# Fewer VectorE instructions ahead of the three accumulations in step 23 of each expert, and the two parts of k and v added before the fold's transposes

## The chip, the core and the metric

One core of a Trainium2 chip runs the whole program. Its engines are TensorE (PE, with its weight loads PEld), VectorE (DVE), ScalarE (ACT), GpSimd (POOL) and SyncE (SP, which issues the DMAs). The metric is the device time of one execution in microseconds (us); of several runs the median is given.

## The reference, cut to what matters

Attention over 32 memory slots per head, and then a mixture of four dense experts on its output:

```python
a = softmax(phi)                                  # over the sequence, 8 batches x 8 heads
k_m = einsum('bhsm,bhsd->bhmd', a, k)             # 32 x 64 per head
v_m = einsum('bhsm,bhsd->bhmd', a, v)
attn = softmax(scale * q @ k_m^T)                 # over the 32 slots
x = (attn @ v_m), heads side by side              # 4608 x 512
p = domain_probs / domain_probs.sum(-1)
out = sum over e of p[:, e] * (relu(x @ w1[e]) @ w2[e])   # 4 experts, 512 -> 1024 -> 512
```

## The kernel before

Every large product is made from two parts of each operand, a rounded "hi" and the rest "lo" (hi*hi + hi*lo + lo*hi). ACT writes a hi with a copy that rounds; DVE then writes the lo as the difference.

**The main loop.** The batches are taken in four pairs (k). For each pair and each of four experts (e) there are 32 steps: 16 for the even batch, 16 for the odd one, each in two halves of the sequence with eight steps (j = 0 to 7, one for each 128 of the expert's 1024 hidden columns). That makes 512 steps; "step 23" below is the eighth and last step of the odd batch's first half, in each of the 16 blocks of 32. In a step PE runs `first_mm(s + 2)`, the six products of the first layer of two steps ahead (lines 416 to 418, tile `p1`, shown as `p`), then the side work that was planned for the step, then `second(s)`, three products for each output tile of 128 tokens (lines 457 to 459, tile `p2`, also shown as `p`). ACT (L432) and DVE (L438) turn `p1` into `h`, or into `hm` for the 64 tokens that the two batches share.

**The output tiles.** A half has two output tiles, the odd batch's first half three (t0 = 5, 6 and 4). A tile collects its products over eight steps in one of four PSUM buffers (tag `p2`), and at j = 7 DVE adds it, times the token's probability, to `acc` or `accm` (L474; L472 for the first expert). The buffers are taken in turn: tile 8, which begins in step 24 as the second tile there, takes the buffer of tile 5, which ends in step 23. DVE runs its instructions in the order written, so tile 5's accumulation comes after all side work that was planned for DVE in step 23.

**Side work.** Meanwhile the next expert's weights are split (`w`, L597/601 and L625/629), the products of v and w1 are made and split (`pv` at L360 to 362, `vw` at L372 by ACT and L378 by DVE), and the attention of later batches runs. A planner writes this order: every operation has an engine, a cost and the operations that it depends on; `place` puts it into the first step in which `room(eng, s)` holds what is already there and its cost (in PE columns), one step later than anything it needs from another engine. `BUSY` names steps of a block (22 to 31) in which attention work is not put. Within a step, up to a cost of 2300, DVE's side work stands ahead of the step's `h` (only what needs nothing of another engine in that step), and the rest behind it; the accumulations are last.

**The fold.** For batches 2 to 7, `kv_ops` leaves for each pair of heads (hp) a PSUM tile `x` of 128 rows by 256 columns: two parts (hi and lo of the softmax weights), each for two heads, as rows; k and v as columns. `kv_out` scales and copies it to SBUF (`xs`, ACT, L234). `kv_fold` turns it with PE transposes (L244, tile `kvp`), four for two head pairs (one group, g). `kv_pick_ops` takes the blocks that are wanted: two copies of the first part into `kvT` (L920, one on ACT, one on DVE), and two additions of the second part (L925, DVE). There are two groups in each of six batches, twelve in all. Batches 0 and 1 use `kv_out`, `kv_fold` and `kv_pick`, and are scheduled by hand.

Of the kernel before, what the change touches and what calls it, by code (L numbers as in the profile page):

```python
# [9 lines left out]
F32 = mybir.dt.float32  # L10
F32R = mybir.dt.float32r
AF = mybir.ActivationFunctionType
ALU = mybir.AluOpType
# [3 lines left out]
B, H, S, D, M = 8, 8, 576, 64, 32  # L17
N, DM, E, F = 4608, 512, 4, 1024
P = 128
# [4 lines left out]
NJ = F // P  # L24
# [5 lines left out]
STAGE = 5  # L30
TH = S // 2
KVS = 2
AHEAD = 2


# [12 lines left out]
def body(ctx: ExitStack, tc: tile.TileContext, qm, qt, qh, kv, kvt, phi, phn, prob, w1, w2, out):  # L48
    nc = tc.nc
    pool = lambda name, **k: ctx.enter_context(tc.tile_pool(name=name, bufs=1, **k))  # L50
    const, wp, work, att = pool("const"), pool("wp"), pool("work"), pool("att")
    psum = pool("psum", space=PSUM)

    ident = const.tile([P, P], F32, name="ident")
    make_identity(nc, ident)
    kvT = [const.tile([P, 2, NP, 2 * M], F32, name=f"kvT{i}") for i in range(2)]
# [74 lines left out]
    st = {}  # L131
# [71 lines left out]
    def kv_split(b, hp, raw, c2, eng):  # L203
        tag = {"tag": "kvs", "bufs": KVS} if b else {"tag": "vw1", "bufs": 5}
        t = att.tile([P, 4 * TH] if b else [P, 1024], F32R, name="kvs", **tag)
        t = t[:, :1024].rearrange("p (s f) -> p s f", s=2)
        t = t.rearrange("p s (i d) -> p s i d", i=2)
        src = raw[:, 2 * c2:2 * c2 + 2].rearrange("p c w d -> p c (w d)")
        nc.scalar.copy(t[:, 0], src)
        eng.tensor_sub(t[:, 1], src, t[:, 0].bitcast(F32))  # L210
        st["kvs", b, hp, c2] = t
# [16 lines left out]
        )  # L228

    def kv_out(b, hp):  # L230
        xs = att.tile([P, 2 * P], F32, name="xs", tag="xs", bufs=2)
        x = st["x", b, hp // 2][:, hp % 2, :]
        if b > 1:
            nc.scalar.activation(xs, x, AF.Copy, scale=st["rz", b][:, hp:hp + 1])  # L234
        else:
            nc.scalar.copy(xs, x)
        st["xs", b, hp] = xs

    def kv_fold(b, hp):
        g = hp // 2  # L240
        if hp % 2 == 0:
            st["kvp", b, g] = psum.tile([P, 2, 2, P], F32, name="kvp", tag="pm", bufs=4)
        for w in range(2):
            nc.tensor.transpose(  # L244
                st["kvp", b, g][:, hp % 2, w, :], st["xs", b, hp][:, w * P:(w + 1) * P], ident
            )
# [154 lines left out]
    def where(s):  # L401
        k, s = divmod(s, PAIR)
        e, s = divmod(s, STEPS)
        odd, s = divmod(s, 2 * NJ)
        half, j = divmod(s, NJ)
        return k, e, odd, half, j
# [14 lines left out]
    def first_hi(s, ps):  # L421
        _, _, odd, _, j = where(s)
        h = work.tile([P, 2, 2 * P], F32R, name="h", tag="h", bufs=AHEAD + 2)
        parts = [(h, slice(0, 2 * P), slice(0, 2 * P))]
# [91 lines left out]
    OA = lambda n, fn, *deps, **k: Op("ACT", 350 + 1.9 * n, fn, deps, **k)  # L516
    OD = lambda n, fn, *deps, **k: Op("DVE", 290 + 2.42 * n, fn, deps, **k)
    OG = lambda n, fn, *deps, **k: Op("POOL", 300 + 2 * n, fn, deps, **k)
    OT = lambda n, fn, *deps, **k: Op("PE", n, fn, deps, **k)
# [5 lines left out]
    def room(eng, s):  # L525
        odd, half, j = where(s)[2:]
        n = HALF[odd][half]
        wide, tiles_ = n == WIDE, 2 + (odd == 1 and half == 0)
        length = 6 * n + 3 * DM * tiles_ + used["PE", s]
        if eng == "PE":  # L530
            return 2400
        if eng == "POOL":
            return 3000
        if eng == "SP":
            return 4
        if eng == "ACT":
            return 0.95 * length - 840 - 470 * wide
        done = (3 if odd == 1 and half == 1 else 2) if j == 0 else 0
        return 0.95 * length - 910 - 445 * wide - 1640 * done

    busy = [True]

# [13 lines left out]
    def place(ops, lo=MANUAL, bank=None):  # L556
        while True:
            done, after = [], defaultdict(int)
            for op in ops:
                s = max([op.lo, lo, MANUAL, after[op.eng]] + [d.step + lag for d, lag in op.deps])  # L560
                while not fits(op, s):
                    s += 1
                op.step = after[op.eng] = s
                charge(op, s)
                done.append(op)
            span = range(ops[bank[0]].step, ops[bank[1]].step + 1) if bank else ()
            if all(banks[s] < 2 and not (busy[0] and s % STEPS in BUSY) for s in span):
                break
            for op in done:
                charge(op, op.step, -1)  # L570
            lo = max(lo, ops[0].step) + 1
        for s in span:
            banks[s] += 1
        for op in ops:
            todo[op.step][op.eng].append(op)
            assert op.late is None or op.step <= op.late
        return ops
# [9 lines left out]
        def give(self, op):  # L587
            self.last.append(op)

    w1_ring, kvs_ring = Ring(4), Ring(KVS)  # L590

    def plan_w1(e, fh, g, lo):
        key = ("w1", e, fh, g)
# [47 lines left out]
    last, VTS = {}, {}  # L641
# [15 lines left out]
    def prev(name, lag=1):  # L657
        d = last.get(name)
        return d and (d, lag)

    def plan_att(b, lo):
# [99 lines left out]
        def kv_ops(hp):  # L761
            key = ("kv", b, hp)

            def k_hi(c2):
                t = att.tile([P, 4 * TH], F32R, name="kvs", tag="kvs", bufs=KVS)
                t = t[:, :1024].rearrange("p (s i d) -> p s i d", s=2, i=2)
# [22 lines left out]
        at_kv = max(lo, lw[0].step - 2)  # L789
        for g in range(2):  # L790
            u = kv_ops(2 * g)
            u += kv_ops(2 * g + 1)
            us = u if g == 0 else us + u
            xa = [OA(256, lambda i=i, g=g: kv_out(b, 2 * g + i), u[-1], prev("fold")) for i in range(2)]
            place(u + xa, at_kv, (4, len(u) + 1))
            last["x"] = u[-1]
            f = OT(512, lambda g=g: [kv_fold(b, 2 * g + i) for i in range(2)], xa[1])
            pk = kv_pick_ops(b, g, f)
            place([f] + pk, 0, (0, len(pk)))
            last["fold"] = f  # L800
        last["a"] = last["tail"] = u[-1]
        last["rz"] = xa[1]

        v = []
        for par in range(2):
            a_ = OA(128, lambda par=par: vt_hi(b, par), pk[-1])
            v += [a_, OD(128, lambda par=par: vt_lo(b, par), a_)]
        place(v)
        zero = OG(512, lambda: kz_zero(b), (u[-1], 1))
# [1 line left out]
        for par in range(2):  # L811
            a_ = OA(128, lambda par=par: kz_hi(b, par), zero, pk[-1])
# [5 lines left out]
        def st_ops(g, half):  # L818
            key = ("qh", b, g, half)

            def q_hi():
                q = att.tile([P, 4 * TH], F32R, name="qs", tag="kvs", bufs=KVS)
                st["q", b, g, half] = q.rearrange("p (s i t) -> p s i t", s=2, i=2)
# [36 lines left out]
        for g in range(2):  # L860
# [23 lines left out]
            def s_turn(g=g, box=box):  # L884
                if g == 0:
                    st["AT", b] = att.tile([P, 2, 2, S], F32R, name="AT", tag="AT", bufs=3)
                box["t"] = att.tile([P, 4 * TH], F32, name="at_t", tag="kvs", bufs=KVS)[:, :S]
                nc.vector.transpose(box["t"], box["e"])
# [9 lines left out]
            c = [OD(S, s_max, outs[g]), OD(S, s_sub)]  # L898
            c += [OA(S, s_exp, c[1])]
            c += [OD(S + 200, s_sum, c[2]), OD(S, s_mul)]  # L900
            ready = (b - 3) // 2 * PAIR + PAIR - (2 * NJ if (b - 3) % 2 == 0 else 0) - AHEAD
            c += [OD(S, s_turn, c[4], kvs_ring.take(), lo=ready)]
# [4 lines left out]
            last[f"at{g}"] = c[5]  # L907
        need = k * PAIR + (2 * NJ if b % 2 else 0) - AHEAD
        assert c[-1].step < need, (b, c[-1].step, need)

    def kv_pick_ops(b, g, f):
        def sl(i):
            return slice(64 * i, 64 * i + 64), slice(M * i, M * i + M)

        kvd = kvT[b % 2][:, :, 2 * g:2 * g + 2]
        kvp = lambda: st["kvp", b, g].rearrange("p h w c -> p w h c")

        def copy(i, op):
            r, m = sl(i)
            op(kvd[r, :, :, m], kvp()[r, :, :, m])  # L920

        def add(i):
            r, m = sl(i)
            lo = slice(2 * M + M * i, 2 * M + M * i + M)
            nc.vector.tensor_add(kvd[r, :, :, m], kvd[r, :, :, m], kvp()[r, :, :, lo])  # L925

        p0 = OA(128, lambda: copy(0, nc.scalar.copy), f)
        p1 = OD(128, lambda: copy(1, nc.vector.tensor_copy), f)
        p2 = OD(128, lambda: add(1), p1)
        return [p0, p1, p2, OD(128, lambda: add(0), p0)]  # L930

    def vt_at(b, par):
        k, odd = b // 2, b % 2
# [4 lines left out]
    def vt_hi(b, par):  # L938
        if ("vt", b // 2) not in st:
            st["vt", b // 2] = att.tile([P, NP, 2, P], F32R, name="vt", tag="vt", bufs=2)  # L940
        dst, src = vt_at(b, par)
        nc.scalar.copy(dst[:, :, 0, :], src)
# [48 lines left out]
    def run_step(s):  # L991
        todo_s, ahead = todo[s], s + AHEAD < LAST
        run_plan(s)
        for op in todo_s["SP"]:
            emit(op)
        if ahead:
            ps = first_mm(s + AHEAD)
        before, after = cut(todo_s["ACT"], 1400, s)
        for op in before:
            emit(op)  # L1000
        if ahead:
            parts = first_hi(s + AHEAD, ps)
        for op in after + todo_s["POOL"]:
# [41 lines left out]
    with tc.manual_schedule():  # L1045
# [30 lines left out]
        for hp in range(2):  # L1076
            kv_out(0, hp)
# [94 lines left out]
```

## Time and profile before

| what | value |
|---|---|
| median of 3 runs | 1406.05 us (1405.99 to 1406.14) |
| the profiled execution's own time | 1406.91 us |
| its span, first to last instruction | 1405.1 us |
| busy: PE, PEld | 1392.0 us, 1216.2 us |
| busy: DVE, ACT, POOL | 883.5 us, 636.9 us, 31.5 us |
| TensorE clock granted, mean | 0.998 |

In the profile a row of a group gives the line, the engine, the operation, the tile written and those read, the shapes and the count, then busy time and mean duration, then the engine's idle time before these instructions with what ended it. A row of the waits gives who waited, for whom, the total, how often, and the longest. A row of the timeline gives start and duration in us, the engine, the line, and how many instructions in succession it stands for. PE's instructions overlap, so what one costs is the distance between starts, not its duration.

### The profile page before, as it was taken

The numbers are of one execution on the slowest core, as the hardware profiler recorded it, in microseconds if no ns is written. First come the engines' busy times: TensorE is split into PE (matmuls) and PEld (weight loads), VectorE is DVE, ScalarE is ACT, GpSimd is POOL, SyncE is SP. The second block draws the span as 40 slices with busy tenths as digits, with TensorE's granted clock in tenths as the row PEclk, the third lists the DMA queues.
The fourth block names the chain that finished last, engine by engine and source line by source line (L and its number), as shares of the span: only waits on it lengthen the run. The fifth ranks groups of instructions, "written<-read, shape, count | busy, mean of one in ns | idle before, by whom it ended". The sixth has DMA issues, their size and how long they took to land.

```text
span 1405.1 us, 20419 instructions
## 1 busy us (share of the span) xinstructions
PE 1392.0 (99%) x7612; PEld 1216.2 (87%) x7612; DVE 883.5 (63%) x1883; ACT 636.9 (45%) x1579; POOL 31.5 (2%) x39
## 2 busy tenths in 40 slices
PE   8999999999999999999999999999999999999998
PEld 7888888888888888888888888888888888888887
DVE  7777556686676756767665665766767454463732
ACT  7645444464445545445343454544535243342521
POOL 4300000000000000000000000000000000000000
PEclk9999999999999999999999999999999999999999
DMA  6622221222522222321322223232222111121001
GB/s 238 212 79 86 97 91 49 87 98 92 161 76 95 75 69 77 120 91 41 115 99 80 89 71 105 63 105 85 72 97 91 53 37 60 46 75 45 1 31 38
DMA packets 37683, 119.10 MB, mean 85 GB/s; under 512 B 4176, under 2 KB 4560, under 8 KB 37584
## 3 DMA queue, kind: packets, MB, share of 16 engines
q1 hardware_dynamic: 37584, 117.79, 25.8%
q8 instruction: 60, 0.98, 0.3%
q14 instruction: 39, 0.32, 0.1%
HBM read 108.34 MB, written 9.44 MB: 84 GB/s over the span
## 4 chain that ended last, share of the span: by engine, by line
PE 95%; DVE 3%; ACT 1%; issue 0%; DMA 0%; SPq 0%; DVEq 0%; ACTq 0%
PE p L457 19%; PE p L458 18%; PE p L459 18%; PE p L418 9%; PE p L416 9%; PE p L417 9%; PE x L221 2%; PE pv L360 2%; PE pv L361 2%; PE pv L362 2%; PE sT L834 1%; DVE vw L378 1%; PE sc L299 1%; DVE w L601 1%; DVE acc L474 1%; PE kvp L244 1%
## 5 line engine op out<-in xcount | busy, mean ns | idle before, releaser
L432 ACT ACTIVATE h<-p 128x256 fp32r<-128x256 f32 x512 | 196.0, 383 | 510.6 <-PE p L418 470.4
L438 DVE SCALAR_TENSOR_TENSOR h<-p,h 128x256 fp32r<-128x256 f32 x512 | 215.3, 420 | 327.1 <-ACT h L432 183.3
L457 PE MATMUL p<-w,h 128*128 128x512 f32 x1024 | 404.5, 395 | 2.4 <-DVE acc L474 1.3
L458 PE MATMUL p<-w,h 128*128 128x512 f32 x1024 | 403.6, 394 | 0.0
L459 PE MATMUL p<-w,h 128*128 128x512 f32 x1024 | 401.4, 392 | 0.0
L416 PE MATMUL p<-AT,vw 128*128 128x256 f32 (+1 forms) x1024 | 303.2, 296 | 0.0
L417 PE MATMUL p<-AT,vw 128*128 128x256 f32 (+1 forms) x1024 | 302.3, 295 | 0.6 <-DVE AT L352 0.6
L418 PE MATMUL p<-AT,vw 128*128 128x256 f32 (+1 forms) x1024 | 302.1, 295 | 0.3 <-DVE vw L378 0.3
L459 PEld LDWEIGHTS p<-w,h 128*128 128x128 f32 x1024 | 192.2, 188 | 42.8
L457 PEld LDWEIGHTS p<-w,h 128*128 128x128 f32 x1024 | 192.3, 188 | 36.5 <-DVE acc L474 5.9
L458 PEld LDWEIGHTS p<-w,h 128*128 128x128 f32 x1024 | 192.6, 188 | 27.0 <-DVE w L109 0.4
L417 PEld LDWEIGHTS p<-AT,vw 128*128 128x128 f32 x1024 | 193.6, 189 | 21.9 <-DVE AT L352 0.8
L416 PEld LDWEIGHTS p<-AT,vw 128*128 128x128 f32 x1024 | 192.5, 188 | 21.3
L418 PEld LDWEIGHTS p<-AT,vw 128*128 128x128 f32 x1024 | 192.7, 188 | 0.8 <-DVE vw L378 0.5
L378 DVE TENSOR_TENSOR vw<-pv,vw 64x512 fp32r<-64x512 f32 x254 | 174.9, 689 | 17.5 <-ACT vw L372 13.2
L372 ACT CAST vw<-pv 64x512 fp32r<-64x512 f32 x254 | 146.9, 578 | 20.8 <-PE pv L362 17.5
L432 ACT ACTIVATE hm<-p 128x64 fp32r<-128x64 f32 x256 | 56.6, 221 | 200.3 <-PE p L418 199.6
L438 DVE SCALAR_TENSOR_TENSOR hm<-p,hm 128x64 fp32r<-128x64 f32 x256 | 56.0, 219 | 142.3 <-ACT h L432 142.2
L601 DVE TENSOR_TENSOR w<-stage,w 128x512 fp32r<-128x512 f32 x120 | 80.7, 679 | 0.6
L629 DVE TENSOR_TENSOR w<-stage,w 128x512 fp32r<-128x512 f32 x120 | 80.0, 681 | 0.5
L597 ACT CAST w<-stage 128x512 fp32r<-128x512 f32 x120 | 73.8, 624 | 0.8
L625 ACT CAST w<-stage 128x512 fp32r<-128x512 f32 x120 | 73.0, 622 | 0.7
(125 smaller groups left out, 1200.6 us busy)
## 6 DMA issues: line engine op xcount, KB each, us to landing
stage<-in_w SPq DMA_DIRECT2D x132, 512.0 KB, 3.5
stage<-in_kv SPq DMA_DIRECT2D x32, 512.0 KB, 3.6
out<-acc SPq DMA_DIRECT2D x32, 256.0 KB, 2.1
stage<-in_qh SPq DMA_DIRECT2D x24, 288.0 KB, 2.9
ph<-in_phi SPq DMA_DIRECT2D x16, 288.0 KB, 4.3
stage<-in_kvt SPq DMA_DIRECT2D x8, 512.0 KB, 3.5
pn<-in_phn SPq DMA_DIRECT2D x6, 640.0 KB, 3.9
stage<-in_qm SPq DMA_DIRECT2D x4, 512.0 KB, 4.0
```

The lines of the kernel that those rows point to most:

```text
L372: nc.scalar.copy(vw[c, odd, fh, hp // 2][r, 0, :], ps[r])
L378: nc.vector.tensor_sub(t[r, 1, :], ps[r], t[r, 0, :].bitcast(F32))
L416: nc.tensor.matmul(ps, w[:, 0, f], at_t[:, g, 0, c], start=g == 0, stop=False)
L417: nc.tensor.matmul(ps, w[:, 0, f], at_t[:, g, 1, c], start=False, stop=False)
L418: nc.tensor.matmul(ps, w[:, 1, f], at_t[:, g, 0, c], start=False, stop=g == 1)
L432: nc.scalar.activation(t[:, 0, to], ps[:, at_], AF.Relu)
L438: nc.vector.scalar_tensor_tensor(t[:, 1, to], ps[:, at_], 0.0, t[:, 0, to].bitcast(F32), ALU.max, ALU.subtract)
L457: nc.tensor.matmul(po[t], x[:, 0, :], w[:, 0, :], start=j == 0, stop=False)
L458: nc.tensor.matmul(po[t], x[:, 0, :], w[:, 1, :], start=False, stop=False)
L459: nc.tensor.matmul(po[t], x[:, 1, :], w[:, 0, :], start=False, stop=j == NJ - 1)
L601: nc.vector.tensor_sub(t[:, 1, :], raws[key][:, i, :], t[:, 0, :].bitcast(F32))
L629: nc.vector.tensor_sub(t[:, 1, :], raws[key][:, i, :], t[:, 0, :].bitcast(F32))
```

## The change

There are two parts.

**Room.** `room` offers DVE 2400 less in a step with three output tiles and j = 7, which is step 23. Its room falls from 4847 to 2447 where PE has no side work there. A split of 512 columns has a cost of 1529, so one fits where three did.

**Fold.** For batches 2 to 7, `kv_cross` (ACT) scales the second part of each head's rows and writes it to `xt` on the 64 partitions of the first part of the same head; `kv_sum` (DVE) scales the first part and adds `xt`, into `xs`. One `xs` then holds the sums for two head pairs, on its two halves of the partitions. `kv_turn` (PE) needs two transposes for a group in place of four, and `kv_place` copies two blocks to `kvT` (one on ACT, one on DVE); the two additions are gone. `xs` and `xt` come from the tag of the former `xs`, two buffers, which are made 288 columns wide (`XS`) instead of 256.

```diff
+XS = 288
...
     def kv_out(b, hp):
-        xs = att.tile([P, 2 * P], F32, name="xs", tag="xs", bufs=2)
+        xs = att.tile([P, XS], F32, name="xs", tag="xs", bufs=2)[:, :2 * P]
         x = st["x", b, hp // 2][:, hp % 2, :]
-        if b > 1:
-            nc.scalar.activation(xs, x, AF.Copy, scale=st["rz", b][:, hp:hp + 1])
-        else:
-            nc.scalar.copy(xs, x)
+        nc.scalar.copy(xs, x)
...
         done = (3 if odd == 1 and half == 1 else 2) if j == 0 else 0
-        return 0.95 * length - 910 - 445 * wide - 1640 * done
+        early_ = 2400 if tiles_ == 3 and j == NJ - 1 else 0
+        return 0.95 * length - 910 - 445 * wide - 1640 * done - early_
...
-            xa = [OA(256, lambda i=i, g=g: kv_out(b, 2 * g + i), u[-1], prev("fold")) for i in range(2)]
-            place(u + xa, at_kv, (4, len(u) + 1))
-            last["x"] = u[-1]
-            f = OT(512, lambda g=g: [kv_fold(b, 2 * g + i) for i in range(2)], xa[1])
-            pk = kv_pick_ops(b, g, f)
-            place([f] + pk, 0, (0, len(pk)))
-            last["fold"] = f
+            xt = [xs_ring.take(), xs_ring.take()]
+            xa = [OA(256, lambda i=i, g=g: kv_cross(b, 2 * g + i), u[-1], xt[0]) for i in range(2)]
+            xd = [OD(256, lambda i=i, g=g: kv_sum(b, 2 * g + i), xa[i], xt[1]) for i in range(2)]
+            place(u + xa + xd, at_kv, (4, len(u) + 3))
+            f = OT(256, lambda g=g: kv_turn(b, g), xd[1])
+            xs_ring.give(xd[1])
+            xs_ring.give(f)
+            pk = [
+                OA(128, lambda g=g: kv_place(b, g, 0, nc.scalar.copy), f),
+                OD(128, lambda g=g: kv_place(b, g, 1, nc.vector.tensor_copy), f),
+            ]
+            place([f] + pk, 0, (0, 2))
...
+    def kv_cross(b, hp):
...
+        nc.scalar.activation(
+            st["xt", b][to, :2 * P], st["x", b, hp // 2][at_, i, :], AF.Copy,
+            scale=st["rz", b][at_, hp:hp + 1],
+        )
+    def kv_sum(b, hp):
...
+        nc.vector.scalar_tensor_tensor(
+            st["xs", b][r, :2 * P], st["x", b, hp // 2][r, i, :], st["rz", b][r, hp:hp + 1],
+            st["xt", b][r, :2 * P], ALU.mult, ALU.add,
+        )
+    def kv_turn(b, g):
+        st["kvp", b, g] = psum.tile([P, 2, P], F32, name="kvp", tag="pm", bufs=4)
+        for w in range(2):
+            nc.tensor.transpose(
+                st["kvp", b, g][:, w, :], st["xs", b][:, w * P:(w + 1) * P], ident
+            )
+    def kv_place(b, g, i, op):
+        r, m = slice(64 * i, 64 * i + 64), slice(M * i, M * i + M)
+        kvp = st["kvp", b, g].rearrange("p w (h c) -> p w h c", h=2)
+        op(kvT[b % 2][r, :, 2 * g:2 * g + 2, m], kvp[r, :, :, m])
```

What this does to the order of the instructions is seen at three places.

The first is DVE around step 23 of the block with pair 1 and its second expert. The rows before begin with the `h` that is made in step 23 and end with those of steps 24 and 25:

```order
L438 SCALAR_TENSOR_TENSOR h<-p_5624,h 128x256
L378 TENSOR_TENSOR vw<-pv,vw 64x512 x2
L601 TENSOR_TENSOR w_5606<-stage,w_5606 128x512
L474 SCALAR_TENSOR_TENSOR acc<-p_5416,pt,acc 128x512
L474 SCALAR_TENSOR_TENSOR acc<-p_5420,pt,acc 128x512
L474 SCALAR_TENSOR_TENSOR accm<-p_5424,pt,accm 128x512
L438 SCALAR_TENSOR_TENSOR h<-p_5653,h 128x256
L601 TENSOR_TENSOR w_5635<-stage,w_5635 128x512
L438 SCALAR_TENSOR_TENSOR h<-p_5671,h 128x256
```

The same place in the changed kernel (its line numbers are two or one lower here):

```order
L436 SCALAR_TENSOR_TENSOR h<-p_5618,h 128x256
L376 TENSOR_TENSOR vw<-pv,vw 64x512
L472 SCALAR_TENSOR_TENSOR acc<-p_5402,pt,acc 128x512
L472 SCALAR_TENSOR_TENSOR acc<-p_5406,pt,acc 128x512
L472 SCALAR_TENSOR_TENSOR accm<-p_5410,pt,accm 128x512
L436 SCALAR_TENSOR_TENSOR h<-p_5645,h 128x256
L376 TENSOR_TENSOR vw<-pv,vw 64x512
L436 SCALAR_TENSOR_TENSOR h<-p_5663,h 128x256
L600 TENSOR_TENSOR w_5597<-stage,w_5597 128x512
L600 TENSOR_TENSOR w_5629<-stage,w_5629 128x512
```

One `vw` and one `w` that stood ahead of the accumulations now stand behind them, in step 25, where the second `w` already was. The same is so in 14 of the 16 blocks. Of the other two, the third block of the program loses one `w` from step 23, and the last has no side work.

The second place is PE in steps 7 and 8 of a block in which batch 3 is folded. Before, in step 7:

```order
L418 MATMUL p_3432<-AT,vw 128x320
L244 MATMUL kvp<-ident,xs 128x128 x4
L457 MATMUL p_3284<-w_3267,h 128x512
L458 MATMUL p_3284<-w_3267,h 128x512
L459 MATMUL p_3284<-w_3267,h 128x512
```

In the changed kernel, in step 8:

```order
L416 MATMUL p_3453<-AT,vw 128x320
L938 MATMUL kvp<-ident,xs 128x128 x2
L455 MATMUL p_3469<-w_2945,h 128x512
L456 MATMUL p_3469<-w_2945,h 128x512
L457 MATMUL p_3469<-w_2945,h 128x512
```

Two transposes are gone, and the other two come one step later, since a DVE instruction now stands between `x` and the transposes.

The third place is DVE around the second fold of the same batch. Before, from the turn of the scores (`at_t`) in step 15 to the fold's copies and additions:

```order
L888 STREAM_TRANSPOSE at_t<-st 128x576
L438 SCALAR_TENSOR_TENSOR h<-p_3605,h 128x256
L438 SCALAR_TENSOR_TENSOR hm<-p_3605,hm 128x64
L920 COPY kvT_76<-kvp 64x2x2x32
L925 TENSOR_TENSOR kvT_76<-kvT_76,kvp 64x2x2x32
```

And in the changed kernel:

```order
L892 STREAM_TRANSPOSE at_t<-st 128x576
L930 SCALAR_TENSOR_TENSOR xs<-x,rz,xt 64x256 x2
L436 SCALAR_TENSOR_TENSOR h<-p_3598,h 128x256
L436 SCALAR_TENSOR_TENSOR hm<-p_3598,hm 128x64
L898 TENSOR_TENSOR AT<-at_t,AT 128x576
L436 SCALAR_TENSOR_TENSOR hm<-p_3622,hm 128x64
L436 SCALAR_TENSOR_TENSOR h<-p_3622,h 128x256
L898 TENSOR_TENSOR AT<-at_t,AT 128x576
L945 COPY kvT_76<-kvp 64x2x2x32
```

The two sums stand ahead of the step's `h`, the copy to `kvT` comes a step later than before, and no addition follows it. SP's queue keeps its loads; a few loads of `w`, `qh` and `pn` change places with their neighbours, as the steps of the instructions that free their buffers moved.

More of the change, by code (lines that the diff above doesn't have):

```diff
@@ L588, in give @@
             self.last.append(op)
-    w1_ring, kvs_ring = Ring(4), Ring(KVS)
+    w1_ring, kvs_ring, xs_ring = Ring(4), Ring(KVS), Ring(2)
     def plan_w1(e, fh, g, lo):
@@ L793, in plan_att @@
             us = u if g == 0 else us + u
-            xa = [OA(256, lambda i=i, g=g: kv_out(b, 2 * g + i), u[-1], prev("fold")) for i in range(2)]
-            place(u + xa, at_kv, (4, len(u) + 1))
-            last["x"] = u[-1]
-            f = OT(512, lambda g=g: [kv_fold(b, 2 * g + i) for i in range(2)], xa[1])
-            pk = kv_pick_ops(b, g, f)
-            place([f] + pk, 0, (0, len(pk)))
-            last["fold"] = f
+            xt = [xs_ring.take(), xs_ring.take()]
[10 more added lines that the diff above has]
+            place([f] + pk, 0, (0, 2))
         last["a"] = last["tail"] = u[-1]
-        last["rz"] = xa[1]
+        last["rz"] = xd[1]
         v = []
         for par in range(2):
-            a_ = OA(128, lambda par=par: vt_hi(b, par), pk[-1])
+            a_ = OA(128, lambda par=par: vt_hi(b, par), *pk)
             v += [a_, OD(128, lambda par=par: vt_lo(b, par), a_)]
@@ L909, in plan_att @@
         assert c[-1].step < need, (b, c[-1].step, need)
[L911 to L930, printed above, removed]
+    def kv_cross(b, hp):
+        if hp % 2 == 0:
+            st["xt", b] = att.tile([P, XS], F32, name="xt", tag="xs", bufs=2)
+        i = hp % 2
+        to, at_ = slice(64 * i, 64 * i + 64), slice(64 - 64 * i, 128 - 64 * i)
+        nc.scalar.activation(
[3 more added lines that the diff above has]
+    def kv_sum(b, hp):
+        if hp % 2 == 0:
+            st["xs", b] = att.tile([P, XS], F32, name="xs", tag="xs", bufs=2)
+        i = hp % 2
+        r = slice(64 * i, 64 * i + 64)
+        nc.vector.scalar_tensor_tensor(
[12 more added lines that the diff above has]
+        op(kvT[b % 2][r, :, 2 * g:2 * g + 2, m], kvp[r, :, :, m])
     def vt_at(b, par):
```

## The prediction

> **What bounds the kernel now.** I read the page first (span, busy time, the chain that ended last), then the waits, then the timeline of PE and DVE where PE waits.
>
> ```profile
> span 1405.1 us, 20419 instructions
> PE 1392.0 (99%) x7612; PEld 1216.2 (87%) x7612; DVE 883.5 (63%) x1883; ACT 636.9 (45%) x1579; POOL 31.5 (2%) x39
> PE 95%; DVE 3%; ACT 1%; issue 0%; DMA 0%; SPq 0%; DVEq 0%; ACTq 0%
> ```
>
> PE is the bound nearly everywhere: 95% of the last chain. DVE and ACT have slack, so work moved onto them costs nothing unless PE waits for it. The time changes only if PE gets fewer products or shorter waits. DVE's 3% of the chain is what to look for, and among the waits these end at PE in the main loop:
>
> ```profile
> PEld p L457 <- DVE acc L474: 5.9, 10, 0.6
> PEld p L457 <- DVE acc L472: 2.4, 4, 0.6
> PE p L457 <- DVE acc L474: 1.3, 8, 0.2
> PE p L457 <- DVE acc L472: 0.7, 4, 0.2
> ```
>
> The weight load ahead of a second-layer product waits 10 + 4 = 14 times for an accumulation, 0.6 us at the longest and (5.9 + 2.4) / 14 = 0.59 us on the average. Fourteen is the number of blocks in which the change takes two instructions from DVE ahead of step 23's accumulations. One of these places in PE's timeline, steps 23 to 26 of the block whose order is shown above:
>
> ```profile
> 633.30 0.39 PE L459 MATMUL p<-w,h 128*128 128x512 f32 x1
> ...
> 635.65 0.40 PE L457 MATMUL p<-w,h 128*128 128x512 f32 x1
> 635.88 0.40 PE L458 MATMUL p<-w,h 128*128 128x512 f32 x1
> 636.12 0.39 PE L459 MATMUL p<-w,h 128*128 128x512 f32 x1
> 636.68 0.50 PE L457 MATMUL p<-w,h 128*128 128x512 f32 x1 [0.18 <-DVE acc L474]
> 637.02 0.40 PE L458 MATMUL p<-w,h 128*128 128x512 f32 x1
> ...
> 640.99 0.40 PE L360 MATMUL pv<-w,vt 128*128 128x512 f32 x1
> ```
>
> And DVE over the same time:
>
> ```profile
> 633.51 0.42 DVE L438 SCALAR_TENSOR_TENSOR h<-p,h 128x256 fp32r<-128x256 f32 x1 [1.50 <-ACT h L432]
> 633.97 1.39 DVE L378 TENSOR_TENSOR vw<-pv,vw 64x512 fp32r<-64x512 f32 x2
> 635.29 0.67 DVE L601 TENSOR_TENSOR w<-stage,w 128x512 fp32r<-128x512 f32 x1
> 635.89 1.39 DVE L474 SCALAR_TENSOR_TENSOR acc<-p,pt,acc 128x512 f32<-128x512 f32 x2
> 637.21 0.73 DVE L474 SCALAR_TENSOR_TENSOR accm<-p,pt,accm 128x512 f32<-128x512 f32 x1
> 637.87 0.41 DVE L438 SCALAR_TENSOR_TENSOR h<-p,h 128x256 fp32r<-128x256 f32 x1
> 638.20 0.67 DVE L601 TENSOR_TENSOR w<-stage,w 128x512 fp32r<-128x512 f32 x1
> 638.87 0.42 DVE L438 SCALAR_TENSOR_TENSOR h<-p,h 128x256 fp32r<-128x256 f32 x1
> ```
>
> Tile 5's last product starts at 633.30 and lasts 0.39, so it can be accumulated from about 633.7. DVE gets to it at 635.89, behind two `vw` and one `w`; its first accumulation ends near 636.6, and at 636.68 PE starts tile 8 in that buffer. Undisturbed, these products start 0.23 us apart (635.65, 635.88, 636.12), so L458 would have come at 636.58. It came at 637.02: 0.44 us lost.
>
> **Part 1, the room in step 23.** One `vw` and one `w` leave the stretch ahead of the accumulations: 0.70 + 0.67 = 1.37 us of DVE by the rows above (the two `vw` take 1.39 together). The accumulation of tile 5 then begins near 634.6 and ends near 635.3. PE loads the weights of a product while the one before runs, so the buffer must be free at about 636.1; there is 0.8 us to spare, and the wait goes whole, not in part. A control stands in the trace. In the program's third block PE has side work in step 23 too, which makes the step longer; the accumulation of tile 5 ends there near 288.7, 1 us before PE needs the buffer, and PE does not wait (first row DVE, the others PE in step 24):
>
> ```profile
> 287.99 1.40 DVE L474 SCALAR_TENSOR_TENSOR acc<-p,pt,acc 128x512 f32<-128x512 f32 x2
> ...
> 289.73 0.39 PE L459 MATMUL p<-w,h 128*128 128x512 f32 x1
> 289.95 0.39 PE L457 MATMUL p<-w,h 128*128 128x512 f32 x1
> ```
>
> L457 follows after 0.22 us there. What one wait costs in the other blocks lies between 0.44 us and that of the shortest that I found:
>
> ```profile
> 889.92 0.39 PE L459 MATMUL p<-w,h 128*128 128x512 f32 x1
> 890.43 0.50 PE L457 MATMUL p<-w,h 128*128 128x512 f32 x1
> 890.76 0.39 PE L458 MATMUL p<-w,h 128*128 128x512 f32 x1
> ```
>
> 0.84 us from L459 to L458, less two distances of 0.23, is 0.38 us. The sum is between 14 x 0.38 = 5.3 and 14 x 0.44 = 6.2 us. Since the average wait of the weight load, 0.59, is close to its longest, I take 14 x 0.425 = 5.9 us.
>
> Where do the moved instructions go? Into step 25, ahead of and behind its `h`. DVE after the change: accumulations from 634.6 to about 636.7, the `h` of step 24 to 637.1, `vw` to 637.8. That `vw` frees the buffer of its product, and by the order of waits PE's `pv` of step 26 now waits for it. It stands at 640.99 in the trace, and so at about 640.55 without the loss: 2.7 us later than the release. The `h` of step 25 comes near 638.9 as before, and the two `w` behind it fill DVE to about 640.6. That `h` is needed by PE in step 27, after the whole of step 26, whose `pv` stands at 640.99: over 2 us later. So the cover is a step of PE or more, and I cost the move at nothing; if it is gone, the next thing late is the `pv` of step 26. ACT's order in steps 23 to 25 is the same.
>
> **Part 2, the fold.** A block of four transposes and one of two (`nb`, the same kind of transpose for the softmax's scale), each with the product before and the two behind:
>
> ```profile
> 498.30 0.31 PE L418 MATMUL p<-AT,vw 128*128 128x320 f32 x1
> 498.44 0.60 PE L244 MATMUL kvp<-ident,xs 128*128 128x128 f32 x4
> 498.80 0.48 PE L457 MATMUL p<-w,h 128*128 128x512 f32 x1
> 499.11 0.40 PE L458 MATMUL p<-w,h 128*128 128x512 f32 x1
> ...
> 149.86 0.38 PE L681 MATMUL nb<-ident,nm 128*128 128x128 f32 x2
> 150.00 0.48 PE L457 MATMUL p<-w,h 128*128 128x512 f32 x1
> 150.31 0.39 PE L458 MATMUL p<-w,h 128*128 128x512 f32 x1
> ```
>
> From the first transpose to L458 it is 0.67 us with four and 0.45 us with two: 0.22 us for two, 0.11 us each. Two are removed in each of twelve groups: 24 x 0.11 = 2.6 us. PE had no wait in such a block, so this comes off the bound in full.
>
> The side that replaces them, from the groups:
>
> ```profile
> L244 PE MATMUL kvp<-ident,xs 128*128 128x128 f32 x64 | 9.7, 275 | 0.0
> L234 ACT ACTIVATE xs<-x,rz 128x256 f32<-128x256 f32 x24 | 11.4, 476 | 4.3 <-PE x L224 4.2
> L925 DVE TENSOR_TENSOR kvT<-kvT,kvp 64x128 f32<-64x128 f32 x24 | 6.8, 283 | 0.5
> L438 DVE SCALAR_TENSOR_TENSOR h<-p,h 128x256 fp32r<-128x256 f32 x512 | 215.3, 420 | 327.1 <-ACT h L432 183.3
> ```
>
> ACT keeps 24 activations of 256 columns, on half the partitions: 11.4 us as now. DVE loses 24 additions (6.8 us) and gets 24 sums of 64x256; the trace has none, the nearest row is `h`, the same operation on the same 256 columns from PSUM, 0.42 us, so 10.1 us; from the addition's 0.28 (6.8 us) to double that of `h` (20 us) as bounds. DVE is busier by 3 us, between 0 and 13, in a span in which it idles 327 us ahead of the `h` rows alone. That idle time, 0.64 us a step on the average, covers most of the 0.84 us of a pair of sums, and `h` is made two steps ahead of its use. The transposes now wait for DVE instead of ACT, but the sums stand ahead of the `h` of their step, and the transposes come in the next one, behind six products (six times 0.15 us by 498.30 and 498.44): nothing, or at worst 0.84 - 0.64 = 0.2 us in each of twelve groups, 2.4 us, where the sums don't fit the idle time. `kvT` comes one step later; the `vt`, `kz` and scores behind it move with it and stay steps ahead of their users. The wider `xs` and the neighbours that change places in SP's queue I cost at nothing: DMA has 0% of the chain.
>
> **The Trainium skill on transposes.** The row of `kvp` shows 275 ns for one, but the starts are 0.11 us apart, and only the distance is saved. The Trainium skill, page "TensorE: Matmul & The Clock Gate", section "Part 4: PE-mode transpose", gives about 275 ns for a 128x128 transpose in a kernel, most of it access latency. The duration agrees with the row, though as a price it would give an estimate of 24 x 0.275 = 6.6 us, 4 us more than the trace's distances; by that rule the time would be 1393.5, and the two blocks above speak against it.
>
> **Sum.** 5.9 + 2.6 = 8.5 us less. Against the profiled execution, 1406.91 becomes 1398.4; it stood 0.86 above the median of 1406.05, so the median becomes **1397.5 us**, 0.6% faster. A measurement of this kernel tells about 0.2% (2.8 us) from no change.
>
> **Rivals.**
> - The wait only moves, from the accumulation to the `vw` that now holds a product's buffer into step 25, at about the same price. For: a new wait of PE on DVE in each of these blocks. Against: the 2.7 us worked out above. Then only the transposes count: 1406.05 - 2.6 = 1403.4, which is not told from the same.
> - Half of the waits stay, since DVE comes later into step 23 where steps 21 and 22 got more work. For: one more `w` in step 22 of some blocks. Against: the 1.50 us that DVE idled ahead of 633.51. 1397.5 + 3.0 = 1400.5.
> - A transpose is worth its whole duration: 24 x 0.275 = 6.6 instead of 2.6, so 1393.5. Against: the distances.
> - Slower: the sums become the bound of the fold. If DVE has a backlog at that point, PE stands at the transposes until both sums are done. It decides from (8.5 + 2.8) / 12 = 0.94 us for each group; with the two sums in full (0.84), their hand-over and the rest of an `h` (0.42 at most), some 1.2 us x 12 = 14.4 us, the time is 1406.05 - 8.5 + 14.4 = 1412. For: PE now waits there for an engine that is 63% busy. Against: the sums have a step's start to themselves, with 0.9 us of products behind it before they are needed.
>
> **How the numbers follow.** The forecast 0.78: by its bounds 5.3 to 6.2 and 2.6, from 1397.3 to 1398.2, and with the 0.2 us a group up to 1400.6. Half of the waits 0.08, the wait that moves 0.06, whole durations 0.05, slower 0.03. The range from 1396.0 to 1401.0 holds the first two. Faster by over 0.2% (below 1403.2) are the forecast, half the waits and whole durations: 0.91; the moved wait is within it: 0.06; slower 0.03.
>
> **What would show it.** Right: no row of PE or PEld waiting for `acc` in the main loop; step 24's L457 of the second tile 0.23 us behind L459; 0.45 us from the first `kvp` transpose to L458; 40 `kvp` transposes (64 - 24); DVE busy at about 887. Wrong: a row of PE waiting for `vw`, `xs` or `kvT`, or `acc` rows left with shorter waits.

## The result, and the profile after

| kernel | median | runs |
|---|---|---|
| before, same chip | 1406.1 us | 1405.59 to 1407.0, 6 runs |
| changed | 1397.66 us | 1397.28 to 1397.87, 6 runs |

The changed kernel takes 0.9939 of the time before, 95% interval 0.9926 to 0.9952: 8.4 us less, 0.6%. The forecast was 1397.5 us. One execution of the first experiment below (e1), at a mean granted clock of 0.654 and 1950.3 us, is left out of every number. The profiled execution took 1397.32 us. From its page, the span, the busy time and the shares of the chain that ended last:

```profile
span 1395.5 us, 20389 instructions
PE 1383.7 (99%) x7588; PEld 1212.9 (87%) x7588; DVE 887.6 (64%) x1883; ACT 639.4 (46%) x1579; POOL 31.0 (2%) x39
PE 98%; DVE 1%; DMA 1%; ACT 0%; issue 0%; SPq 0%; DVEq 0%; ACTq 0%
```

DVE's share of the chain fell from 3% to 1%, and PE's rose from 95% to 98%. PE's busy time fell by 8.3 us (1392.0 to 1383.7). Of that only the transposes, 2.6 us, are work that is gone. Some 2 us lie in the first 62 us (below), where PE took longer for the same products before. The rest, 3.7 us, had been waiting that the page counts as busy: of the 0.44 us lost at a wait only 0.18 is shown as idle, since a product that waits for its buffer is shown with 0.50 us instead of 0.39, and the products around it lie further apart.

Of the four rows of waits for `acc` none is left at PE or PEld. The only row of the waits that still names `acc` itself has the two sides reversed, DVE waiting for PE, as one row did before too (2.6 us, once):

```profile
DVE acc L472 <- PE p L457: 3.0, 2, 2.6
```

The place that the prediction showed, first DVE (633.51 to 639 before), then PE and its weight loads at step 24, where tile 8 takes over the buffer of tile 5:

```profile
629.37 0.69 DVE L376 TENSOR_TENSOR vw<-pv,vw 64x512 fp32r<-64x512 f32 x1
630.09 1.41 DVE L472 SCALAR_TENSOR_TENSOR acc<-p,pt,acc 128x512 f32<-128x512 f32 x2
631.42 0.74 DVE L472 SCALAR_TENSOR_TENSOR accm<-p,pt,accm 128x512 f32<-128x512 f32 x1
632.08 0.41 DVE L436 SCALAR_TENSOR_TENSOR h<-p,h 128x256 fp32r<-128x256 f32 x1
632.41 0.67 DVE L376 TENSOR_TENSOR vw<-pv,vw 64x512 fp32r<-64x512 f32 x1
633.82 0.42 DVE L436 SCALAR_TENSOR_TENSOR h<-p,h 128x256 fp32r<-128x256 f32 x1 [0.74 <-ACT h L430]
634.16 1.28 DVE L600 TENSOR_TENSOR w<-stage,w 128x512 fp32r<-128x512 f32 x2
```
```profile
631.51 0.39 PE L457 MATMUL p<-w,h 128*128 128x512 f32 x1
631.73 0.39 PE L455 MATMUL p<-w,h 128*128 128x512 f32 x1
631.96 0.40 PE L456 MATMUL p<-w,h 128*128 128x512 f32 x1
...
635.94 0.40 PE L358 MATMUL pv<-w,vt 128*128 128x512 f32 x1
```
```profile
631.51 0.19 PEld L455 LDWEIGHTS p<-w,h 128*128 128x128 f32 x1
```

One `vw` now stands ahead of the accumulations instead of two and a `w`. One accumulation takes some 0.74 us (the row of `accm`), so that of tile 5 ends near 630.83, and the weight load of tile 8 starts at 631.51, 0.7 us later, with no wait. The products follow each other after 0.22 and 0.23 us. The `vw` that was moved ends at 633.08, and the `pv` that takes its product's buffer starts at 635.94, 2.9 us later. Behind that `vw` DVE is idle for 0.74 us, waiting for ACT: the moved work went into idle time.

The fold, from the groups; L938 are the transposes of the main loop, L242 those of batches 0 and 1, which didn't change:

```profile
L930 DVE SCALAR_TENSOR_TENSOR xs<-x,rz,xt 64x256 f32<-64x256 f32 x24 | 11.4, 477 | 0.2
L920 ACT ACTIVATE xt<-x,rz 64x256 f32<-64x256 f32 x24 | 11.3, 471 | 5.7 <-PE x L225 5.3
L938 PE MATMUL kvp<-ident,xs 128*128 128x128 f32 x24 | 4.6, 271 | 0.0
L242 PE MATMUL kvp<-ident,xs 128*128 128x128 f32 x16 | 2.5, 280 | 0.0
```

And one of the twelve groups in the timeline, DVE's two sums and PE:

```profile
325.39 0.97 DVE L930 SCALAR_TENSOR_TENSOR xs<-x,rz,xt 64x256 f32<-64x256 f32 x2
```
```profile
327.28 0.31 PE L416 MATMUL p<-AT,vw 128*128 128x320 f32 x1
327.43 0.38 PE L938 MATMUL kvp<-ident,xs 128*128 128x128 f32 x2
327.56 0.48 PE L455 MATMUL p<-w,h 128*128 128x512 f32 x1
327.88 0.40 PE L456 MATMUL p<-w,h 128*128 128x512 f32 x1
```

From the first transpose to L456 it is 0.45 us, as long as the pair of `nb` transposes took. PE doesn't wait: the sums end at 326.36, the transposes start at 327.43.

The two profiled executions lie 9.6 us apart (1406.91 and 1397.32), 1.2 more than the medians. About 1 us of it is no part of the change. The first 62 us, in which PE runs the same products in both kernels, in the windows (span of the window, then busy time and count of PE, PEld, DVE, ACT, POOL, then the granted clock, the DMA share and GB/s), first after, then before:

```profile
0.00:62.00 62.00, 54.12 (x334) 47.00 (x335) 51.74 (x114) 44.42 (x98) 25.02 (x25) 0.97 0.66 234
```
```profile
0.00:62.00 62.00, 55.14 (x327) 47.93 (x328) 51.29 (x111) 43.54 (x96) 25.37 (x25) 0.94 0.65 229
```

At a granted clock of 0.97 instead of 0.94, PE had done 7 products more by then. At 0.15 us from one first-layer product to the next, an estimate from the starts above, that is 1 us.

So the kernels are better compared behind this head. Up to the program's third accumulation every engine runs the same instructions in the same order in both kernels; all that the change adds, drops or moves comes later. It starts here, first after, then before:

```profile
89.21 1.39 DVE L470 TENSOR_SCALAR acc<-p,pt 128x512 f32<-128x512 f32 x2
```
```profile
90.11 1.39 DVE L472 TENSOR_SCALAR acc<-p,pt 128x512 f32<-128x512 f32 x2
```

From there to the end of the span it is 1395.5 - 89.2 = 1306.3 us after and 1405.1 - 90.1 = 1315.0 us before: 8.7 us less, where the forecast had 8.5. For the experiments the same distance, from the profiled execution of each, is called "behind the head".

### The profile page after: what moved, and what is told of

Read it like the earlier page. It is cut to its first block, busy times and chain, and to the rows that moved or that the text cites. A ratio compares the mean times of both kernels' runs of the same rounds, so it can differ in the third digit from the quotient of the medians.

```text
span 1395.5 us, 20389 instructions
## 1 busy us (share of the span) xinstructions
PE 1383.7 (99%) x7588; PEld 1212.9 (87%) x7588; DVE 887.6 (64%) x1883; ACT 639.4 (46%) x1579; POOL 31.0 (2%) x39
## 4 chain that ended last, share of the span: by engine, by line
PE 98%; DVE 1%; DMA 1%; ACT 0%; issue 0%; SPq 0%; DVEq 0%; ACTq 0%
PE p L456 19%; PE p L457 19%; PE p L455 19%; PE p L414 10%; PE p L416 10%; PE p L415 10%; PE pv L358 2%; PE pv L359 2%; PE x L222 2%; PE pv L360 2%; PE sT L838 1%; PE sc L297 1%; DMA stage<-in_kv 1%; PE x L225 0%; PE kvp L938 0%
## 5 line engine op out<-in xcount | busy, mean ns | idle before, releaser
L456 PE MATMUL p<-w,h 128*128 128x512 f32 x1024 | 403.7, 394 | 0.0
L455 PE MATMUL p<-w,h 128*128 128x512 f32 x1024 | 403.2, 394 | 0.2 <-ACT h L430 0.2
L457 PE MATMUL p<-w,h 128*128 128x512 f32 x1024 | 401.4, 392 | 0.0
L416 PE MATMUL p<-AT,vw 128*128 128x256 f32 (+1 forms) x1024 | 302.0, 295 | 0.4 <-DVE vw L376 0.3
L457 PEld LDWEIGHTS p<-w,h 128*128 128x128 f32 x1024 | 192.2, 188 | 42.8
L455 PEld LDWEIGHTS p<-w,h 128*128 128x128 f32 x1024 | 192.3, 188 | 28.9 <-ACT h L430 0.4
L456 PEld LDWEIGHTS p<-w,h 128*128 128x128 f32 x1024 | 192.6, 188 | 27.4 <-DVE w L110 0.4
L416 PEld LDWEIGHTS p<-AT,vw 128*128 128x128 f32 x1024 | 192.7, 188 | 0.9 <-DVE vw L376 0.5
```

The costliest lines, as they stand in the source:

```text
L416: nc.tensor.matmul(ps, w[:, 1, f], at_t[:, g, 0, c], start=False, stop=g == 1)
L455: nc.tensor.matmul(po[t], x[:, 0, :], w[:, 0, :], start=j == 0, stop=False)
L456: nc.tensor.matmul(po[t], x[:, 0, :], w[:, 1, :], start=False, stop=False)
L457: nc.tensor.matmul(po[t], x[:, 1, :], w[:, 0, :], start=False, stop=j == NJ - 1)
```

## The experiments

The theory is that of the prediction, and the rivals were put against one part of it each. The kernel before ran on the same chips at medians of 1405.99 us (e1, e2, e3, e5), 1406.2 us (e4, e6, e7, e8) and 1406.24 us (e9, e1b).

**e1, the room alone.** The kernel before, with the room's two lines:

```diff
+        early_ = 2400 if tiles_ == 3 and j == NJ - 1 else 0
+        return 0.95 * length - 910 - 445 * wide - 1640 * done - early_
```

> The kernel before with the smaller room in step 23 alone; the fold as before. Theory (the wait for tile 5's accumulation goes whole, a transpose is worth the 0.11 us between starts): 14 x 0.43 = 6.0 us less than 1406.1, so 1400.1 us, no row of PE waiting for acc in the main loop, 64 kvp transposes. Rival (a transpose is worth its whole duration, 24 x 0.27 = 6.5 us of the 8.4 measured): the room brings the other 1.9 us, so 1404.2.

Four of the five executions took 1399.8 to 1401.2 us, with a median of 1400.59; ratio 0.996 (0.9946 to 0.9973), which is 3.8 to 7.6 us less than before. A second run of it, for the profile:

> The smaller room alone again, for its profile. Theory: 1400.1 to 1400.7; no row of TensorE waiting for acc in the main loop, and 64 transposes into kvp as before, with the fold's two pairs per group apart.

1399.83 us in its one execution, 0.3 below what was expected. The chain by engine, from its page, and the transposes of the fold, from its groups:

```profile
PE 98%; DVE 1%; ACT 0%; issue 0%; DMA 0%; DVEq 0%; ACTq 0%
```
```profile
L244 PE MATMUL kvp<-ident,xs 128*128 128x128 f32 x64 | 9.7, 274 | 0.0
```

The 64 transposes are there, and no row of PE or PEld waiting for `acc`. The room alone is worth 5.4 us by the medians (6.4 by the one run), and 5.9 behind the head (1309.1 against 1315.0 us). The rival's 1.9 us lie outside the interval, and so do the 3 us of the prediction's rival by which half of the waits stay.

**e2, the fold alone.** The changed kernel without those two lines.

> The changed kernel with the old room in step 23; the new fold alone. Theory: 24 x 0.11 = 2.6 us less than before, 1403.5 us, with the 14 waits of about 0.43 us back. Rival (whole durations): 6.5 us less, 1399.6. Second rival (the two parts are one, the fold's gain needs the free DVE): 1406.

1403.8 us, ratio 0.9983 (0.9974 to 0.9992): 2.2 us less than before, and 2.6 behind the head (1312.4 us). Both rivals, 1399.6 and 1406 us, lie outside the interval. The waits are back:

```profile
PEld p L455 <- DVE acc L472: 6.0, 10, 0.6
PEld p L455 <- DVE acc L470: 2.4, 4, 0.6
PE p L455 <- DVE acc L472: 1.7, 10, 0.2
PE p L455 <- DVE acc L470: 0.6, 4, 0.2
```

10 + 4 waits of 0.6 us on the average, the numbers of the kernel before. Hardly any action of the parts on each other shows: 5.4 + 2.2 = 7.6 us against 8.4 measured together, within the intervals (3.8 to 7.6 us for the room, 1.1 to 3.7 for the fold), and behind the head 5.9 + 2.6 = 8.5 us against 8.7.

**e3, two operations ahead of the accumulations instead of one.** The changed kernel with a deduction that leaves room for two splits:

```diff
-        early_ = 2400 if tiles_ == 3 and j == NJ - 1 else 0
+        early_ = 1500 if tiles_ == 3 and j == NJ - 1 else 0
```

> The changed kernel with room for two splits in step 23 instead of one (1500 taken off instead of 2400). In the changed kernel tile 5's accumulation ends at 630.84 in the block shown, and the weight load of tile 8 begins at 631.51: 0.67 us to spare, one more split takes 0.66 to 0.68. Theory (a threshold: PE loses only what is late at that point): 0 to 0.1 us in each of 14 blocks, 1397.7 to 1399.1. Rival (PE's loss grows with each split ahead, half of it back for half the splits): 14 x 0.215 = 3.0 us more, 1400.7.

1397.08 us (1396.78 to 1399.01), ratio 0.9938 (0.9926 to 0.9951), as the changed kernel; behind the head both take 1306.3 us. The rival's 1400.7 lies outside the interval, and no row of PE or PEld waits for `acc`. The same place, DVE and the weight load of tile 8:

```profile
631.03 1.39 DVE L376 TENSOR_TENSOR vw<-pv,vw 64x512 fp32r<-64x512 f32 x2
632.35 1.39 DVE L472 SCALAR_TENSOR_TENSOR acc<-p,pt,acc 128x512 f32<-128x512 f32 x2
633.66 0.73 DVE L472 SCALAR_TENSOR_TENSOR accm<-p,pt,accm 128x512 f32<-128x512 f32 x1
```
```profile
633.18 0.19 PEld L455 LDWEIGHTS p<-w,h 128*128 128x128 f32 x1
```

The accumulation of tile 5 ends near 633.08 (632.35 + 0.73), 0.1 us ahead of the load, and that is enough. It is a threshold: with one or two operations ahead PE loses nothing, with three 0.4 us per block.

**e5, nothing taken out of step 23, only put behind.** The kernel before, where in step 23 DVE's side work is written behind the accumulations:

```diff
-        for op in after + todo_s["PE"]:
+        behind = after if s % STEPS == 23 else []
+        for op in after[len(behind):] + todo_s["PE"]:
             emit(op)
         second(s)
+        for op in behind:
+            emit(op)
```

> The kernel before; in step 23 alone the side work on DVE behind the step's h is written behind the three accumulations instead of ahead of them. No instruction leaves the step. Theory (it is what stands ahead of tile 5's accumulation, not how much DVE has in the step): the 14 waits go, 1400.1 us as with the room alone. Rival (DVE has too much work in steps 23 and 24, wherever it stands): the wait comes back as one for vw or h, 1404 to 1406.

1399.67 us (1399.55 to 1399.86), ratio 0.9953 (0.9941 to 0.9966), with no row of PE or PEld waiting for `acc`, and 1309.1 us behind the head, as with the room alone. The rival's 1404 to 1406 falls. DVE does the same work in the same step, in another order, and the whole of the room's gain is there. It is the order ahead of the accumulations that cost, not the amount of work in the step.

**e9, the fold with that order.** The changed kernel, with the old room and e5's edit.

> The changed kernel's fold, the room of before, and in step 23 VectorE's side work written behind the step's accumulations instead of ahead of them. Theory (either cure takes away the same 14 waits of TensorE for acc, and nothing is left to gain behind them): 1397.5, as the changed kernel. Rival (the side work behind the accumulations is worth about 1 us more than a smaller room, as the 1399.67 of that order alone against the 1400.67 of the smaller room alone would have it): 1396.6.

1397.04 us (1396.62 to 1398.08), ratio 0.9934 (0.992 to 0.9948). It lies between the two expectations, 0.6 us below the changed kernel, and their runs overlap. Behind the head e9, e3 and the changed kernel all take 1306.3 us, as e1b and e5 both take 1309.1: the order is worth what the room is worth, and the rival falls.

**e6, three operations more ahead of the accumulations.** The changed kernel, with three maxima over a tile of `acc`, used by nothing, put there in 15 blocks:

```diff
+        if s % STEPS == 23 and s < LAST - STEPS:
+            for _ in range(3):
+                t = att.tile([P, 1], F32, name="idle", tag="idle", bufs=1)
+                nc.vector.reduce_max(t, acc[where(s)[0], 3], AX.X)
         second(s)
```

> The changed kernel with three maxima over 512 columns (about 0.68 us each, result unused) on DVE in step 23, just ahead of the accumulations, in the first 15 blocks. Theory: tile 5's accumulation ends 3 x 0.68 = 2.0 us later, 1.37 us after the weight load of tile 8 would begin; of such lateness PE lost 0.44 of 0.51 us in the kernel before, so 1.3 us in each of 14 blocks and about 0.3 in the third: 18.5 us more, 1416 us. Rival (PE's loss is bounded at about one split, the rest is caught up by work two steps ahead): 14 x 0.43 = 6 us more, 1404.

1417.55 us, ratio 1.0079 (1.0066 to 1.0093): 19.9 us slower than the changed kernel, 20.0 behind the head (1326.3 us). The rival's 1404 falls. The same place, DVE, then PE:

```profile
637.87 2.13 DVE L1030 TENSOR_REDUCE idle<-acc 128x1 f32<-128x512 f32 x3
640.03 1.41 DVE L472 SCALAR_TENSOR_TENSOR acc<-p,pt,acc 128x512 f32<-128x512 f32 x2
```
```profile
639.30 0.39 PE L457 MATMUL p<-w,h 128*128 128x512 f32 x1
640.83 0.50 PE L455 MATMUL p<-w,h 128*128 128x512 f32 x1 [1.14 <-DVE acc L472]
641.17 0.39 PE L456 MATMUL p<-w,h 128*128 128x512 f32 x1
```

From L457 to L456 it is 1.87 us instead of 0.46, so 1.41 us are lost here; 14 such blocks give 19.7 us. (In the third block, the control, PE now waits too and loses 0.36 us: the waits name 15 loads.) DVE's work was made 2.13 us longer with 0.7 us to spare, so the wait costs, to about 0.1 us, what goes past the threshold: 2.13 - 0.7 = 1.4 us.

**e4, more transposes.** The changed kernel, with each pair of transposes made five times (8 more per group, 96 in all):

```diff
-        for w in range(2):
+        for w in [0, 1] * 5:
```

> The changed kernel, with each group's two transposes done five times over into the same tile: 8 more in each of 12 groups, 96 in all. Theory (0.109 us between starts): 10.5 us more than 1397.7, 1408.2 us. Rival (the duration of 0.271 us counts): 26.0 us more, 1423.7.

1408.13 us (1407.52 to 1409.04): 10.47 us above the changed kernel, 0.109 us for each of 96; behind the head it is 10.5 us too. The rival's 1423.7 falls. The transposes in the groups, and one fold in PE's timeline:

```profile
L938 PE MATMUL kvp<-ident,xs 128*128 128x128 f32 x120 | 15.0, 272 | 0.0
```
```profile
329.55 1.25 PE L938 MATMUL kvp<-ident,xs 128*128 128x128 f32 x10
330.56 0.48 PE L455 MATMUL p<-w,h 128*128 128x512 f32 x1
```

Each still lasts 272 ns, and L455 starts 1.01 us behind the first of ten, where it was 0.13 us behind the first of two (327.43, 327.56): 0.11 us for each of the eight. So the price of a transpose here is the distance between starts. The Trainium skill's 275 ns (page "TensorE: Matmul & The Clock Gate", section "Part 4: PE-mode transpose") agrees with the duration in this trace; as a price it would give an estimate of 96 x 0.275 = 26 us, and the run shows 10.5.

**e7, the sums three times.** The changed kernel, each sum made three times:

```diff
-        nc.vector.scalar_tensor_tensor(
+        for _ in range(3):
+            nc.vector.scalar_tensor_tensor(
```

> The changed kernel with each of the 24 sums of the fold done three times over: 48 more, 48 x 0.477 = 22.9 us more of DVE, 1.9 us in each group. Theory (the sums stand a step ahead of the transposes, and DVE idles 0.64 us a step on the average): 1397.7 us, or up to 1 us more. Rival (the fold hangs on DVE; no cover beyond the idle time): (1.9 - 0.64) x 12 = 15 us more, 1413.

1404.21 us (1403.75 to 1405.49), ratio 0.9987 (0.9978 to 0.9996): 6.5 us above the changed kernel, 7.0 behind the head (1313.3 us), which neither side expected. Two rows of its waits, and the group shown above in the timeline, DVE, then PE:

```profile
PE kvp L939 <- DVE xs L931: 5.3, 6, 1.0
PEld p L455 <- DVE acc L472: 0.8, 2, 0.4
```
```profile
325.00 3.05 DVE L931 SCALAR_TENSOR_TENSOR xs<-x,rz,xt 64x256 f32<-64x256 f32 x6
```
```profile
326.89 0.30 PE L416 MATMUL p<-AT,vw 128*128 128x320 f32 x1
328.19 0.41 PE L939 MATMUL kvp<-ident,xs 128*128 128x128 f32 x2 [1.00 <-DVE xs L931]
```

The transposes start 0.14 us after the last sum (325.00 + 3.05 = 328.05). In the changed kernel the gap is 327.43 - 326.36 = 1.07 us, so the sums have 0.93 us to spare at this group. Six take 3.05 - 0.97 = 2.08 us more than two: 1.15 us are lost. L416 to the transposes shows the same, 1.30 us instead of 0.15. Five of the twelve groups are like this one; a sixth, with a gap of 1.69 us before, loses 0.53, and in the others the transposes come so late that the sums are done. With two short waits for `acc` (0.23 us lost at each), 5 x 1.15 + 0.53 + 0.46 = 6.7 us, against the 6.5 and 7.0 measured. So the cover of the sums is 0.9 us at the tightest five groups: enough for two sums, not for six.

**e8, the width of `xs`.** The changed kernel with tiles of 256 columns instead of 288:

```diff
-XS = 288
+XS = 256
```

> The changed kernel with xs and xt 256 columns wide instead of 288. Both theories that the width is only an address: 1397.7 us. Rival (the width matters to how operands lie): a difference of over 1 us.

1397.75 us (1396.82 to 1399.01), ratio 0.9937 (0.9925 to 0.995), and 1306.3 us behind the head. The width does nothing that can be measured.

## Why the prediction was right, point by point

- **The waits for `acc`: right, whole.** All 14 are gone. At the place shown tile 8's first product, in tile 5's buffer, starts 0.22 us behind the product before it (0.23 forecast). The term was 5.9 us; by the medians the room alone gave 5.4 (e1) and the order alone 6.3 (e5), and behind the head each gave 5.9. The time to spare was put at 0.8 us and is 0.7. That the wait "goes whole, not in part" is shown by e3 and e6 from both sides: 0.1 us to spare costs nothing, and 1.4 us too late costs 1.4 us.
- **The moved work costs nothing: right.** The `pv` of step 26 comes 2.9 us behind the `vw` that frees its buffer (2.7 forecast). The rival of the wait that moves has no row: PE has no wait for a `vw` or `w` of DVE that was not there before.
- **The transposes: right.** 0.45 us from the first to L456, 40 transposes left in all, and 0.109 us each when 96 are added. The term was 2.6 us; the fold alone gave 2.2 by the medians (e2), 2.6 behind the head.
- **The side that replaces them: right in the sign, small in the size.** A sum takes 0.477 us, not the 0.42 of `h`, so 24 take 11.4 us instead of 10.1. The activations take 11.3 us, as forecast. DVE is busy 887.6 us (about 887 forecast).
- **The cover of the sums: right for this kernel, but not by the reason given alone.** The prediction gave the six products, 0.9 us, and the idle time of DVE, 0.64 us a step on the average. What decides is the distance from the end of the sums to their transposes at the tightest groups: 1.07 us, of which 0.14 are the hand-over. The slower rival had the right mechanism, and e7 shows it at work, though at half of the groups only: its price was spread evenly over twelve.
- **What was right by luck.** The forecast of 1397.5 and the median of 1397.66 agree within 0.2 us, which is closer than a time is known here: single executions of one kernel lie up to 2.2 us apart (e3: 1396.78 to 1399.01). The profiled ones of e3 and of the changed kernel differ by 1.7 us, all of it in the head (their third accumulations start at 90.89 and 89.21). The sum itself was no luck: 8.5 us forecast and 8.7 behind the head, with each term as forecast.

## What to carry to other kernels

In this kernel, an engine that runs in order holds a buffer for as long as everything written ahead of the instruction that frees it; find the buffer's next user, take the distance from the release to that use, and move side work until it is positive. Here 0.1 us to spare was worth as much as 0.7, and neither the amount of work nor the engine's busy share (63%) told of the wait. What a short PE instruction costs is the distance between starts, and work that is put ahead of it on another engine is free only up to the distance at the tightest place, not at the average one. Where runs differ by a microsecond, compare them from an instruction behind the part that varies: what the medians left open to a microsecond came out to 0.2 us behind the head.

## What the runs showed of the hardware that was not expected

- A late buffer costs PE more than the idle time shown at the product. At e6's place the row shows 1.14 us idle, and 1.41 are lost. Of the rest, 0.11 us are behind the wait: the product that follows starts 0.34 us later (640.83, 641.17) instead of 0.23. The other 0.16 are ahead of it: idle time is counted from the end of the product before, 0.39 us after its start, while the next would have started after 0.23. The same 0.11 us more stands behind the shorter waits before the change (636.68, 637.02).
- Behind a pair of transposes the first 512-column product starts at once, and the delay is in the distance from it to the next: 0.32 us (327.56, 327.88) instead of 0.23.
- An execution can differ by 1 to 2 us from its head alone: with clocks of 0.94 and 0.97 in the first 62 us PE had done 327 and 334 products. The profiled execution of e3 had a granted clock of 0.94 there, 322 products, and took 1399.01 us, 1.9 above its kernel's median. The clock is not all of it: at 0.97, e2 had done 329 products and e1b 336. What else decides the head stays open.
- Behind the head the profiled executions repeat to 0.1 us: 1309.1 us twice (e1b, e5) and 1306.3 four times (changed, e3, e8, e9).
